# Moving transposes from TensorE to DMA and the norm to token rows, from batch 3 on, in a linear-attention plus feed-forward kernel

## Chip, cores, metric

One core of a Trainium2 chip. The metric is device time in microseconds of one execution; medians of several executions are quoted. Lower is better. An execution more than 1.5% above the fastest of the same kernel counts as slow and is left out.

## The reference

Eight batches of 8 heads, 576 tokens, 64 features per head. Attention has no softmax: per head `kv = k^T v`, `out = q kv`, then each token's 64 features are divided by their root mean square and multiplied by a gain. The 512 normed features of each of the 4608 tokens then pass a feed-forward layer of 2048 with a leaky activation.

```python
kv  = einsum('bhsd,bhse->bhde', k, v)
out = einsum('bhsd,bhde->bhse', q, kv)
out = out / sqrt(mean(out*out, -1) + 1e-6) * g_norm
h   = x @ w_in                      # x: 4608 x 512
y   = (max(h,0) + alpha*min(h,0)) @ w_out
```

## The kernel before

The feed-forward part runs in nine windows of 512 tokens. In window `w` the kernel interleaves 16 groups: four matmuls into `h_ps` (first layer), their eviction by ScalarE (`m_sb`) and VectorE (`gt`), and four matmuls into `y_ps` of the window before. After each group, at most a few attention "steps" of window `w + 1` are emitted; I call that place the group's **slot**. Every engine runs its instructions in the order in which they were emitted.

```python
def step_t(b, j):                     # q of a head pair, feature-major, by TensorE
    for t in range(NT):
        nc.tensor.matmul(out=qt_ps[:, t*P:(t+1)*P], lhsT=qs[:, t, 2*j:2*j+2, :],
                         rhs=ident16[:], is_transpose=True, ...)
    nc.vector.tensor_copy(out=qts[b, j][:], in_=qt_ps[:, 0:S])

def step_kv(b, j):                    # five matmuls, then VectorE masks into kvs[b, j]
    ...
def step_ot(w, j):                    # attention output, features on partitions
    nc.tensor.matmul(out=ot_ps[...], lhsT=kvs[b, j][:], rhs=qts[b, j][...], ...)
    nc.scalar.activation(out=sq[:], in_=ot_ps[:], func=AF.Square)

def step_ssq(w, j):                   # sums of squares by a matmul with a mask of ones
    nc.tensor.matmul(out=ssq_ps[:], lhsT=mask16[:], rhs=sq[:], ...)
    # ScalarE: Ln, Exp on 128x512;  VectorE: xts[w, j] = ot_ps * gain * rstd
# ... (cut)
for w in range(1, NW):
    steps = window_steps(w + 1)
    if 1 < w and w + 2 < B:
        load_batch(w + 2); regroup_batch(w + 2)      # GpSimd: loads, then copies
    for g in range(NF):                               # NF = 16
        m1_group(w, g)                                # 4 matmuls + eviction
        # ... y_mm x 4 of window w-1, y_out every fourth group
        want = n * (g - first_g + 1) // (NF - 2 - first_g)
        while steps and n - len(steps) < want:
            steps.pop(0)()                            # the slot
```

Of the kernel before, what the change touches and what calls it, by code (L numbers as in the profile page):

```python
# [9 lines left out]
FP32 = mybir.dt.float32  # L10
FP16 = mybir.dt.float16
AF = mybir.ActivationFunctionType
ALU = mybir.AluOpType
# [4 lines left out]
def kernel(  # L18
# [11 lines left out]
    nc = tc.nc  # L30

    B, H, S, D = q.shape
# [3 lines left out]
    P = 128  # L36
    NPAIR = H // 2
    W = 512
    NW = N_TOK // W
    TPW = W // P  # L40
    TPP = S // P
    MAIN = TPP * P
    REM = S - MAIN
    NT = TPP + 1
    NF = D_FF // P
    NC = D_MODEL // P
    assert NC == NPAIR and 0 < REM < P
    inv_d = 1.0 / D

    const_p = ctx.enter_context(tc.tile_pool(name="constp", bufs=1))  # L50
    w_p = ctx.enter_context(tc.tile_pool(name="weights", bufs=1))
    xt_p = ctx.enter_context(tc.tile_pool(name="xt", bufs=3))
    qkv_p = ctx.enter_context(tc.tile_pool(name="qkv", bufs=1))
    stage_p = ctx.enter_context(tc.tile_pool(name="stage", bufs=2))
    attn_p = ctx.enter_context(tc.tile_pool(name="attn", bufs=2))
# [2 lines left out]
    ps_h = ctx.enter_context(tc.tile_pool(name="psh", bufs=3, space=bass.MemoryType.PSUM))  # L58
    ps_y = ctx.enter_context(tc.tile_pool(name="psy", bufs=1, space=bass.MemoryType.PSUM))
    ps_s = ctx.enter_context(tc.tile_pool(name="pss", bufs=1, space=bass.MemoryType.PSUM))  # L60
    ps_o = ctx.enter_context(tc.tile_pool(name="pso", bufs=2, space=bass.MemoryType.PSUM))
    ps_q = ctx.enter_context(tc.tile_pool(name="psq", bufs=1, space=bass.MemoryType.PSUM))

    ctx.enter_context(
        tc.manual_schedule(engines={ENG.PE, ENG.Activation, ENG.DVE, ENG.Pool, ENG.SP})
# [7 lines left out]
            name=nc.get_next_instruction_name(),  # L73
# [14 lines left out]
    mask16 = const_p.tile([P, P], FP16, name="mask16")  # L88
# [3 lines left out]
    eps_t = const_p.tile([P, 1], FP32, name="eps_t")  # L92
# [3 lines left out]

    alpha_row = const_p.tile([NF, P], FP32, name="alpha_row")
    nc.sync.dma_start(out=alpha_row[:], in_=moe_alpha[:].rearrange("(g p) -> g p", p=P))
    g2col = const_p.tile([P, 1], FP32, name="g2col")
    nc.sync.dma_start(out=g2col[0:64, :], in_=g_norm[:].unsqueeze(1))  # L100
    nc.sync.dma_start(out=g2col[64:128, :], in_=g_norm[:].unsqueeze(1))
# [5 lines left out]
    NBUF = 3  # L107
    bufs = []
    for i in range(NBUF):
        t = {}  # L110
# [22 lines left out]
    def regroup(b, nm, h0, h1, eng=None):  # L133
        dst = bufs[b % NBUF][nm][:, 0:TPP, h0:h1, :].rearrange("p t h d -> p h t d")
        src = stages[b, nm][:, h0:h1, :, :]
        if eng is nc.scalar:
            nc.scalar.copy(out=dst, in_=src)
        else:
            (eng or nc.vector).tensor_copy(out=dst, in_=src)  # L139

    def load_batch(b, names=("k", "v", "q")):
        for nm in names:
            load_rem(b, nm)
            load_main(b, nm, 0, H)

    def regroup_batch(b):
        for nm in ("k", "v", "q"):
            regroup(b, nm, 0, H, nc.gpsimd)
# [24 lines left out]
    def w_in_blk(c, g):  # L173
        i, r = divmod(g, GW)
        return w_in_sb[i][:, c, r * P : (r + 1) * P]
# [22 lines left out]
    def keep_warm(n):  # L198
# [7 lines left out]
        out=alpha_ps[:], lhsT=alpha_row[:], rhs=ident[0:NF, 0:NF], is_transpose=True,  # L206
        start=True, stop=True,
# [4 lines left out]
        out=beta_sb[:], in0=alpha_ps[:], scalar1=-1.0, scalar2=1.0, op0=ALU.mult, op1=ALU.add,  # L212
# [3 lines left out]
    qts, kvs, xts = {}, {}, {}  # L216
# [16 lines left out]
    def step_kv(b, j, pool=(ps_s, "s")):  # L233
        ks, vs = bufs[b % NBUF]["k"], bufs[b % NBUF]["v"]
        kv_ps = pool[0].tile([P, P], FP32, name="kv_ps", tag=pool[1])
        for t in range(NT):
            nc.tensor.matmul(  # L237
                out=kv_ps[:],
                lhsT=ks[:, t, 2 * j : 2 * j + 2, :],
                rhs=vs[:, t, 2 * j : 2 * j + 2, :],  # L240
                start=(t == 0),
                stop=(t == NT - 1),
            )
        kvs[b, j] = attn_p.tile([P, P], FP16, name="kv_sb", tag=f"kv{j}")
        nc.vector.tensor_mul(out=kvs[b, j][:], in0=kv_ps[:], in1=mask32[:])  # L245


    ots = {}

    def step_ot(w, j):  # L250
        ot_ps = ps_o.tile([P, W], FP32, name="ot_ps", tag="o")
        n0 = w * W
        while n0 < (w + 1) * W:
            b = n0 // S
            n1 = min((b + 1) * S, (w + 1) * W)
            nc.tensor.matmul(  # L256
                out=ot_ps[:, n0 - w * W : n1 - w * W], lhsT=kvs[b, j][:],
                rhs=qts[b, j][:, n0 - b * S : n1 - b * S], start=True, stop=True,
            )
            n0 = n1  # L260
        sq = attn_p.tile([P, W], FP16, name="sq_sb")
        nc.scalar.activation(out=sq[:], in_=ot_ps[:], func=AF.Square)  # L262
        ots[w, j] = (ot_ps, sq)

    def step_ssq(w, j):
        ot_ps, sq = ots.pop((w, j))
        ssq_ps = ps_q.tile([P, W], FP32, name="ssq_ps", tag="q")
        nc.tensor.matmul(out=ssq_ps[:], lhsT=mask16[:], rhs=sq[:], start=True, stop=True)  # L268
        rstd = attn_p.tile([P, W], FP32, name="rstd")
        nc.scalar.activation(  # L270
            out=rstd[:], in_=ssq_ps[:], func=AF.Ln, bias=eps_t[:], scale=inv_d,
        )
        nc.scalar.activation(out=rstd[:], in_=rstd[:], func=AF.Exp, bias=0.0, scale=-0.5)  # L273
        xts[w, j] = xt_p.tile([P, W], FP16, name="xt", tag=f"xt{j}")
        nc.vector.scalar_tensor_tensor(  # L275
            out=xts[w, j][:], in0=ot_ps[:], scalar=g2col[:], in1=rstd[:],
            op0=ALU.mult, op1=ALU.mult,
        )

    def window_steps(w):  # L280
        f = []
        for j in range(NPAIR):
            f.append(("t", j))
            if j > 0:
                f.append(("ot", j - 1))
            f.append(("kv", j))
            if j > 0:
                f.append(("ssq", j - 1))
        f += [("ot", NPAIR - 1), ("ssq", NPAIR - 1)]
        if w >= B:  # L290
            f = [x for x in f if x[0] in ("ot", "ssq")]
        fn = {"t": step_t, "kv": step_kv, "ot": step_ot, "ssq": step_ssq}
        return [lambda n=n, j=j: fn[n](w, j) for n, j in f]
# [4 lines left out]
    def m1_mm(h_ps, w, g, cs):  # L298
        for c in cs:
            nc.tensor.matmul(  # L300
                out=h_ps[:], lhsT=w_in_blk(c, g), rhs=xts[w, c][:],
                start=(c == 0), stop=(c == NC - 1),
            )

# [10 lines left out]
    def m1_group(w, g):  # L315
        h_ps = ps_h.tile([P, W], FP32, name="h_ps", tag="h")
        m1_mm(h_ps, w, g, range(NC))
        m1_evac(h_ps, w, g)
# [8 lines left out]
    def y_out(y, w, a):  # L327
        y_sb = ysb_p.tile([P, D_MODEL], FP32, name="y_sb")
        nc.scalar.copy(out=y_sb[:], in_=y[:])  # L329
        i = 0  # L330
        while i < P:
            b, r = divmod(w * W + a * P + i, S)
            if r < MAIN:
                t, p = divmod(r, P)
                cnt = min(P - i, P - p)
                rows = out[b * S : b * S + MAIN, :].rearrange("(p t) m -> t p m", t=TPP)
                dst = rows[t, p : p + cnt, :]
            else:
                cnt = min(P - i, S - r)
                dst = out[b * S + r : b * S + r + cnt, :]  # L340
            nc.sync.dma_start(out=dst, in_=y_sb[i : i + cnt, :])
            i += cnt
# [19 lines left out]
    first = [ps_h.tile([P, W], FP32, name="h_ps", tag="h") for g in range(3)]  # L362
    for g in range(3):
        m1_mm(first[g], 0, g, (0, 1))
    step_ssq(0, 2)
    step_ssq(0, 3)
    for g in range(3):
        m1_mm(first[g], 0, g, (2,))
# [15 lines left out]
    steps = window_steps(1)  # L384
# [8 lines left out]
        f()  # L393

    for w in range(1, NW):
        steps = window_steps(w + 1) if w + 1 < NW else []
        n = len(steps)
        first_g = 4 if w == 1 else 0
        if 1 < w and w + 2 < B:
            load_batch(w + 2)  # L400
            regroup_batch(w + 2)
        y = None
        for g in range(NF):
            if w == 1 and g == first_g - 1:
                for nm in ("q", "k", "v"):
                    regroup(2, nm, 0, H)
                load_batch(3)
                regroup_batch(3)
            m1_group(w, g)
            if w > 1:  # L410
                a, part = divmod(g, TPW)
                if part == 0:
                    y = ps_y.tile([P, W], FP32, name="y_ps", tag="y")
                for gg in range(part * TPW, (part + 1) * TPW):
                    y_mm(y, w - 1, a, gg)
                if part == TPW - 1:
                    y_out(y, w - 1, a)

            want = n * (g - first_g + 1) // (NF - 2 - first_g)
            while steps and n - len(steps) < want:  # L420
                steps.pop(0)()
# [35 lines left out]
```

## Time and profile before

| what | before |
|---|---|
| median time | 329.7 us (329.2 to 330.5, 3 runs) |
| profiled span, clock | 328.0 us, 0.99 |
| TensorE, VectorE, ScalarE, GpSimd busy | 91, 49, 53, 23% |
| one window with a full set of steps | 32.44 us |

How to read it: the lines of the page, and what each of them says, are in the prediction below. A busy share is an average over the whole run; the figure that carries the argument is the issue spacing on TensorE inside one window, read from the timeline.

### The profile page before, as it was taken

What the parts mean: (1) busy time and instruction counts of PE and PEld (TensorE: products, weight loads), DVE (VectorE), ACT (ScalarE), POOL (GpSimd) and SP (SyncE); (2) the same over time, 40 slices, a digit from 0 to 9 for tenths busy, and PEclk for the clock granted to TensorE, in tenths of its full rate; (3) what the DMA queues carried; (4) which work ended last, traced back from release to release, by engine and by line L of the source; (5) the groups of instructions that cost most, each with busy time, mean ns of one, the idle gap of its engine ahead of it and who ended that gap; (6) DMA issues with size and microseconds to landing.
All of it is one profiled execution on the core that took longest, in us unless ns stands there. A gap on an engine that the chain in (4) does not pass through costs nothing.

```text
span 328.0 us, 4205 instructions
## 1 busy us (share of the span) xinstructions
PE 298.4 (91%) x1593; PEld 143.7 (44%) x1593; DVE 160.2 (49%) x271; ACT 173.4 (53%) x291; POOL 74.7 (23%) x80
## 2 busy tenths in 40 slices
PE   5657998768799999999999999999999999999994
PEld 1323354234355545544555455445544444444441
DVE  4247833285665545555455545554555455444300
ACT  2366605635846564657456745674557576544311
POOL 9723442765542055105500000000000000000000
PEclk9999999798999999999999999999999999999999
DMA  7999999996391199109901111101000211000132
GB/s 95 193 203 202 198 195 191 223 145 83 38 178 33 34 126 154 34 33 149 134 32 34 32 32 34 51 13 53 36 23 21 59 38 34 32 32 34 44 86 64
DMA packets 47621, 28.07 MB, mean 86 GB/s; under 512 B 14304, under 2 KB 42992, under 8 KB 47600
## 3 DMA queue, kind: packets, MB, share of 16 engines
q0 software_dynamic: 41904, 18.35, 44.5%
q1 hardware_dynamic: 5696, 9.45, 10.2%
q8 instruction: 12, 0.20, 0.3%
q14 instruction: 9, 0.07, 0.1%
HBM read 36.71 MB, written 9.44 MB: 141 GB/s over the span
## 4 chain that ended last, share of the span: by engine, by line
PE 83%; ACT 7%; DVE 4%; DMA 2%; issue 1%; POOL 1%; POOLq 0%; ACTq 0%
PE h_ps L300 36%; PE y_ps L322 34%; PE kv_ps L237 3%; PE ssq_ps L268 2%; PE qt_ps L222 2%; PE ot_ps L256 2%; ACT rstd L270 2%; DMA qsb<-in_q_dram 2%; ACT rstd L273 2%; DVE xt L275 1%; DVE gt L309 1%; ACT sq_sb L262 1%; ACT m_sb L307 1%; PE yd L322 1%; DVE qt_sb L231 1%
## 5 line engine op out<-in xcount | busy, mean ns | idle before, releaser
L300 PE MATMUL h_ps<-xt,w_in_sb 128*128 128x512 f16 x576 | 147.3, 384 | 4.1 <-ACT y_sb L329 1.5
L309 DVE SCALAR_TENSOR_TENSOR gt<-m_sb,beta_sb,h_ps 128x512 f16<-128x512 f32 x144 | 106.8, 745 | 88.4 <-ACT m_sb L307 86.9
L307 ACT ACTIVATE m_sb<-h_ps 128x512 f32<-128x512 f32 x144 | 85.1, 593 | 83.7 <-PE h_ps L300 83.6
L322 PE MATMUL y_ps<-w_out_sb,gt 128*128 128x512 f16 x512 | 128.8, 379 | 0.0
L322 PEld LDWEIGHTS <-gt 128*128 128x128 f16 x576 | 56.0, 98 | 67.5 <-issue 2.3
L300 PEld LDWEIGHTS <-w_in_sb 128*128 128x128 f16 x576 | 54.9, 99 | 67.2 <-issue 14.5
L275 DVE SCALAR_TENSOR_TENSOR xt<-ot_ps,g2col,rstd 128x512 f16<-128x512 f32 x36 | 27.0, 751 | 46.5 <-ACT rstd L273 46.5
L270 ACT ACTIVATE rstd<-ssq_ps,eps_t 128x512 f32<-128x512 f32 x36 | 24.7, 686 | 18.2 <-PE ssq_ps L268 18.2
L262 ACT ACTIVATE sq_sb<-ot_ps 128x512 f16<-128x512 f32 x36 | 21.3, 597 | 22.6 <-PE ot_ps L256 22.1
L329 ACT COPY y_sb<-y_ps 128x512 f32<-128x512 f32 x32 | 18.7, 585 | 18.4 <-PE y_ps L322 18.4
L273 ACT ACTIVATE rstd<-rstd 128x512 f32<-128x512 f32 x36 | 22.7, 629 | 1.1
L268 PE MATMUL ssq_ps<-sq_sb,mask 128*128 128x512 f16 x36 | 13.6, 378 | 7.0 <-ACT sq_sb L262 5.5
L222 PE MATMUL qt_ps<-ident,qsb 128*128 128x128 f16 x160 | 14.8, 227 | 5.7 <-DVE qsb L139 4.8
L237 PE MATMUL kv_ps<-vsb,ksb 128*128 128x128 f16 x160 | 14.5, 226 | 4.7 <-DVE qt_sb L231 4.7
L222 PEld LDWEIGHTS <-qsb 128*128 128x128 f16 x160 | 11.8, 101 | 13.5 <-DVE qsb L139 5.9
L231 DVE COPY qt_sb<-qt_ps 128x576 f16<-128x576 f16 x32 | 14.3, 451 | 6.4 <-PE qt_ps L222 6.3
L237 PEld LDWEIGHTS <-ksb 128*128 128x128 f16 x160 | 11.9, 101 | 12.1 <-issue 6.1
L256 PE MATMUL ot_ps<-qt_sb,kv_sb 128*128 128x512 f16 (+7 forms) x64 | 14.2, 296 | 0.3 <-DVE kv_sb L245 0.3
L128 POOL DMA_DIRECT2D ksb<-in_k_dram x8 | 5.6, 700 | 36.4 <-PE kv_ps L237 27.8
L139 POOL COPY ksb<-kst 128x2048 f16<-128x2048 f16 x5 | 9.5, 1893 | 18.7 <-DMA kst<-in_k_dram 18.7
L139 POOL COPY qsb<-qst 128x2048 f16<-128x2048 f16 x5 | 9.5, 1894 | 7.4 <-DMA qst<-in_q_dram 7.4
L139 POOL COPY vsb<-vst 128x2048 f16<-128x2048 f16 x5 | 9.5, 1894 | 6.8 <-DMA vst<-in_v_dram 6.8
(44 smaller groups left out, 111.6 us busy)
## 6 DMA issues: line engine op xcount, KB each, us to landing
out_dram<-y_sb SPq DMA_DIRECT2D x40, 128.0 KB, 2.3
out_dram<-y_sb SPq DMA_DIRECT2D x16, 256.0 KB, 2.3
kst<-in_k_dram POOLq DMA_DIRECT2D x7, 512.0 KB, 8.6
vst<-in_v_dram POOLq DMA_DIRECT2D x7, 512.0 KB, 10.1
qst<-in_q_dram POOLq DMA_DIRECT2D x7, 512.0 KB, 12.0
w_in_sb<-in_moe_w_in_dram POOLq DMA_DIRECT2D x4, 512.0 KB, 10.9
w_out_sb<-in_moe_w_out_dram POOLq DMA_DIRECT2D x4, 512.0 KB, 16.5
kst<-in_k_dram POOLq DMA_DIRECT2D x2, 256.0 KB, 5.5
```

The lines of the kernel that those rows point to most:

```text
L139: (eng or nc.vector).tensor_copy(out=dst, in_=src)
L222: nc.tensor.matmul(out=qt_ps[:, t * P : (t + 1) * P], lhsT=qs[:, t, 2 * j : 2 * j + 2, :], rhs=ident16[:], is_transpose=True, start=(t == ...
L237: nc.tensor.matmul(out=kv_ps[:], lhsT=ks[:, t, 2 * j : 2 * j + 2, :], rhs=vs[:, t, 2 * j : 2 * j + 2, :], start=(t == 0), stop=(t == NT - 1),)
L256: nc.tensor.matmul(out=ot_ps[:, n0 - w * W : n1 - w * W], lhsT=kvs[b, j][:], rhs=qts[b, j][:, n0 - b * S : n1 - b * S], start=True, stop=True,
L262: nc.scalar.activation(out=sq[:], in_=ot_ps[:], func=AF.Square)
L270: nc.scalar.activation(out=rstd[:], in_=ssq_ps[:], func=AF.Ln, bias=eps_t[:], scale=inv_d,)
L273: nc.scalar.activation(out=rstd[:], in_=rstd[:], func=AF.Exp, bias=0.0, scale=-0.5)
L275: nc.vector.scalar_tensor_tensor(out=xts[w, j][:], in0=ot_ps[:], scalar=g2col[:], in1=rstd[:], op0=ALU.mult, op1=ALU.mult,)
L300: nc.tensor.matmul(out=h_ps[:], lhsT=w_in_blk(c, g), rhs=xts[w, c][:], start=(c == 0), stop=(c == NC - 1),)
L307: nc.scalar.activation(out=m_sb[:], in_=h_ps[:], func=AF.Relu, scale=-1.0)
L309: nc.vector.scalar_tensor_tensor(out=gt[:], in0=m_sb[:], scalar=beta_sb[:, g : g + 1], in1=h_ps[:], op0=ALU.mult, op1=ALU.add,)
L322: nc.tensor.matmul(out=y[:], lhsT=gts[w, g][:, a * P : (a + 1) * P], rhs=w_out_blk(g), start=(g == 0), stop=(g == NF - 1),)
```

## The change

The intent is to free TensorE of work that is not the feed-forward. From batch 3 on, q is transposed by a DMA; the attention output is computed with tokens on partitions, so that a token's square sum is a row sum on VectorE; GpSimd builds `rstd * gain`; the normed rows go back to feature-major by DMA transposes into `xm`.

```diff
+    NB_PE = 3
-    ps_o = ...(name="pso", bufs=2)   # and ps_q, bufs=1
+    ps_o = ...(name="pso", bufs=1)   # tags o0, o1, o2
+    def transpose_q(b):
+        nc.sync.dma_start_transpose(out=qtms[b][:], in_=bufs[b % NBUF]["q"][:]...)
+    def tile_a(b, t):                 # one tile of 128 tokens, 8 heads
+        ot_ps = ps_o.tile([P, H, D], FP32, tag=f"o{n_tile[0] % 3}")
+        for j in range(NPAIR):
+            nc.tensor.matmul(out=ot_ps[:, 2*j:2*j+2, :], lhsT=qtms[b][:, t*NPAIR+j, :], rhs=kvs[b, j][:])
+        nc.scalar.activation(out=sq[0:n], in_=ot_ps[0:n], func=AF.Square)
+    def tile_b(b, t): ...             # VectorE tensor_reduce: ss
+    def tile_c(b, t): ...             # ScalarE Ln, Exp on 128x8; GpSimd rg = ss * g_all
+    def tile_d(b, t):
+        nc.vector.tensor_mul(out=x[0:n], in0=ot_ps[0:n], in1=rg[0:n])
+        nc.sync.dma_start_transpose(out=xm(w)[:, :, c:c+m], in_=x[i:i+m]...)
... (cut: the tail of batch 2, the list of tiles of a phase)
+            for k, fn in ((3, tile_d), (0, tile_a), (1, tile_b), (2, tile_c)):
+                if 0 <= i - k < len(seq): m.append(fn of seq[i - k])
+            if i < lead: m += first[:cut]           # kv steps, up to two in a slot
...
-        steps = window_steps(w + 1) if w + 1 < NW else []
+        steps = phase_steps(w + 1)
+            if g == NF - 3 and max(w + 2, NB_PE) < B and w + 2 >= NB_PE:
+                transpose_q(w + 2)
```

More of the change, by code (lines that the diff above doesn't have):

```diff
@@ L48 @@
     inv_d = 1.0 / D
+    NB_PE = 3
     const_p = ctx.enter_context(tc.tile_pool(name="constp", bufs=1))
     w_p = ctx.enter_context(tc.tile_pool(name="weights", bufs=1))
-    xt_p = ctx.enter_context(tc.tile_pool(name="xt", bufs=3))
+    xt_p = ctx.enter_context(tc.tile_pool(name="xt", bufs=2))
+    xm_p = ctx.enter_context(tc.tile_pool(name="xm", bufs=3))
     qkv_p = ctx.enter_context(tc.tile_pool(name="qkv", bufs=1))
@@ L60 @@
     ps_s = ctx.enter_context(tc.tile_pool(name="pss", bufs=1, space=bass.MemoryType.PSUM))
-    ps_o = ctx.enter_context(tc.tile_pool(name="pso", bufs=2, space=bass.MemoryType.PSUM))
-    ps_q = ctx.enter_context(tc.tile_pool(name="psq", bufs=1, space=bass.MemoryType.PSUM))
+    ps_o = ctx.enter_context(tc.tile_pool(name="pso", bufs=1, space=bass.MemoryType.PSUM))
     ctx.enter_context(
@@ L98 @@
     nc.sync.dma_start(out=alpha_row[:], in_=moe_alpha[:].rearrange("(g p) -> g p", p=P))
+    g_all = const_p.tile([P, D], FP32, name="g_all")
+    nc.sync.dma_start(out=g_all[:], in_=g_norm[:].partition_broadcast(P))
     g2col = const_p.tile([P, 1], FP32, name="g2col")
@@ L248, with xt_of @@
     ots = {}
+    xms = {}
+    def xt_of(w, c):
+        return xms[w][:, c, :] if w >= NB_PE else xts[w, c][:]
     def step_ot(w, j):
-        ot_ps = ps_o.tile([P, W], FP32, name="ot_ps", tag="o")
+        ot_ps = ps_o.tile([P, W], FP32, name="ot_ps", tag=f"o{j % 2}")
         n0 = w * W
@@ L266, in step_ssq @@
         ot_ps, sq = ots.pop((w, j))
-        ssq_ps = ps_q.tile([P, W], FP32, name="ssq_ps", tag="q")
+        ssq_ps = ps_o.tile([P, W], FP32, name="ssq_ps", tag="o2")
         nc.tensor.matmul(out=ssq_ps[:], lhsT=mask16[:], rhs=sq[:], start=True, stop=True)
@@ L278, in step_ssq, with step_tail_ot @@
         )
+    TAIL = NB_PE * (S - W)
+    JT = min(NPAIR, W // TAIL)
+    def step_tail_ot(i):
+        ot_ps = ps_o.tile([P, JT, TAIL], FP32, name="ot_ps", tag=f"o{i % 2}")
+        for u in range(JT):
+            j = i * JT + u
+            nc.tensor.matmul(
+                out=ot_ps[:, u, :], lhsT=kvs[NB_PE - 1, j][:],
+                rhs=qts[NB_PE - 1, j][:, S - TAIL : S], start=True, stop=True,
+            )
+        sq = attn_p.tile([P, JT, TAIL], FP16, name="sq_sb")
+        nc.scalar.activation(out=sq[:], in_=ot_ps[:], func=AF.Square)
+        ots["tail", i] = (ot_ps, sq)
@@ new lines, in step_tail_ssq @@
+    def step_tail_ssq(i):
+        ot_ps, sq = ots.pop(("tail", i))
+        ssq_ps = ps_o.tile([P, JT, TAIL], FP32, name="ssq_ps", tag="o2")
+        nc.tensor.matmul(out=ssq_ps[:], lhsT=mask16[:], rhs=sq[:], start=True, stop=True)
+        rstd = attn_p.tile([P, JT, TAIL], FP32, name="rstd")
+        nc.scalar.activation(
+            out=rstd[:], in_=ssq_ps[:], func=AF.Ln, bias=eps_t[:], scale=inv_d,
+        )
+        nc.scalar.activation(out=rstd[:], in_=rstd[:], func=AF.Exp, bias=0.0, scale=-0.5)
+        nc.vector.scalar_tensor_tensor(
+            out=xm(NB_PE)[:, i * JT : (i + 1) * JT, 0:TAIL], in0=ot_ps[:], scalar=g2col[:],
+            in1=rstd[:], op0=ALU.mult, op1=ALU.mult,
+        )
@@ new lines, with xm @@
+    qtms, tiles = {}, {}
+    def xm(w):
+        if w not in xms:
+            xms[w] = xm_p.tile([P, NPAIR, W], FP16, name="xm")
+        return xms[w]
+    def transpose_q(b):
+        qtms[b] = attn_p.tile([P, NT * NPAIR, P], FP16, name="qtm")
+        nc.sync.dma_start_transpose(
+            out=qtms[b][:], in_=bufs[b % NBUF]["q"][:].rearrange("p t h d -> p (t h d)"),
+        )
+    n_tile = [0]
+    def tile_a(b, t):
+        ot_ps = ps_o.tile([P, H, D], FP32, name="otm_ps", tag=f"o{n_tile[0] % 3}")
+        n_tile[0] += 1
+        for j in range(NPAIR):
+            nc.tensor.matmul(
+                out=ot_ps[:, 2 * j : 2 * j + 2, :], lhsT=qtms[b][:, t * NPAIR + j, :],
+                rhs=kvs[b, j][:], start=True, stop=True,
+            )
+        n = P if t < TPP else REM
+        sq = attn_p.tile([P, H, D], FP32, name="sqm_sb", tag="rstd")
+        nc.scalar.activation(out=sq[0:n], in_=ot_ps[0:n], func=AF.Square)
+        tiles[b, t] = [n, ot_ps, sq]
@@ new lines, in tile_b, with tile_c @@
+    def tile_b(b, t):
+        n, _, sq = tiles[b, t]
+        ss = attn_p.tile([P, H], FP32, name="ss", bufs=3)
+        nc.vector.tensor_reduce(
+            out=ss[0:n], in_=sq[0:n], op=ALU.add, axis=mybir.AxisListType.X,
+        )
+        tiles[b, t][2] = ss
+    def tile_c(b, t):
+        n, _, ss = tiles[b, t]
+        nc.scalar.activation(
+            out=ss[0:n], in_=ss[0:n], func=AF.Ln, bias=eps_t[0:n], scale=inv_d,
+        )
+        nc.scalar.activation(out=ss[0:n], in_=ss[0:n], func=AF.Exp, bias=0.0, scale=-0.5)
+        rg = attn_p.tile([P, H, D], FP32, name="rg")
+        nc.gpsimd.tensor_tensor(
+            out=rg[0:n], in0=ss[0:n].unsqueeze(2).to_broadcast([n, H, D]),
+            in1=g_all[0:n].unsqueeze(1).to_broadcast([n, H, D]), op=ALU.mult,
+        )
+        tiles[b, t][2] = rg
@@ new lines, in tile_d, with phase_steps @@
+    def tile_d(b, t):
+        n, ot_ps, rg = tiles.pop((b, t))
+        x = attn_p.tile([P, H, D], FP16, name="xrow", bufs=3)
+        nc.vector.tensor_mul(out=x[0:n], in0=ot_ps[0:n], in1=rg[0:n])
+        i = 0
+        while i < n:
+            w, c = divmod(b * S + t * P + i, W)
+            m = min(n - i, W - c)
+            nc.sync.dma_start_transpose(
+                out=xm(w)[:, :, c : c + m], in_=x[i : i + m].rearrange("p h d -> p (h d)"),
+            )
+            i += m
+    def phase_steps(w):
+        if w < NB_PE:
+            return window_steps(w)
+        if w >= NW:
+            return []
+        todo = [(b, t) for b in range(NB_PE, min(B, w + 1)) for t in range(NT)
+                if (b, t) not in done and b * S + t * P < (w + 1) * W]
+        done.update(todo)
+        old = [x for x in todo if x[0] < w]
+        new = [x for x in todo if x[0] == w]
+        pre = []
+        if w == NB_PE:
+            n = NPAIR // JT
+            pre = [lambda i=i: step_tail_ot(i) for i in range(n)] + [
+                lambda i=i: step_tail_ssq(i) for i in range(n)]
+        kv = [lambda j=j: step_kv(w, j) for j in range(NPAIR)] if w < B else []
+        first = []
+        for i in range(max(len(pre), len(kv))):
+            first += kv[i : i + 1] + pre[i : i + 1]
+        seq = old + new
+        lead = len(old)
+        steps = []
+        if lead == 0:
+            steps += [[f] for f in first]
+            first = []
+        for i in range(len(seq) + 3):
+            m = []
+            for k, fn in ((3, tile_d), (0, tile_a), (1, tile_b), (2, tile_c)):
+                if 0 <= i - k < len(seq):
+                    m.append(lambda fn=fn, x=seq[i - k]: fn(*x))
+            if i < lead:
+                cut = -(-len(first) // (lead - i))
+                m += first[:cut]
+                first = first[cut:]
+            steps.append(m)
+        return [lambda m=m: [f() for f in m] for m in steps]
@@ L280, in window_steps @@
+    done = set()
     def window_steps(w):
@@ L300, in m1_mm @@
             nc.tensor.matmul(
-                out=h_ps[:], lhsT=w_in_blk(c, g), rhs=xts[w, c][:],
+                out=h_ps[:], lhsT=w_in_blk(c, g), rhs=xt_of(w, c),
                 start=(c == 0), stop=(c == NC - 1),
```

## The prediction

> **What bounds the kernel now.** I read the page first (busy shares and slices), then the groups, then the waits, then a timeline of one group slot.
>
> ```profile
> PE 298.4 (91%) x1593; PEld 143.7 (44%) x1593; DVE 160.2 (49%) x271; ACT 173.4 (53%) x291; POOL 74.7 (23%) x80
> PE   5657998768799999999999999999999999999994
> POOL 9723442765542055105500000000000000000000
> DMA  7999999996391199109901111101000211000132
> ```
>
> TensorE is at 9 tenths from 90 us to the end, with every other engine near half. The DMA engines are nearly idle in the second half, which is the room that the change wants to use.
>
> ```profile
> L300 PE MATMUL h_ps<-xt,w_in_sb 128*128 128x512 f16 x576 | 147.3, 384 | 4.1 <-ACT y_sb L329 1.5
> L322 PE MATMUL y_ps<-w_out_sb,gt 128*128 128x512 f16 x512 | 128.8, 379 | 0.0
> L275 DVE SCALAR_TENSOR_TENSOR xt<-ot_ps,g2col,rstd 128x512 f16<-128x512 f32 x36 | 27.0, 751 | 46.5 <-ACT rstd L273 46.5
> L268 PE MATMUL ssq_ps<-sq_sb,mask 128*128 128x512 f16 x36 | 13.6, 378 | 7.0 <-ACT sq_sb L262 5.5
> L222 PE MATMUL qt_ps<-ident,qsb 128*128 128x128 f16 x160 | 14.8, 227 | 5.7 <-DVE qsb L139 4.8
> ```
>
> The two big matmul groups wait only 4.1 us in all. Their "mean ns" must not be added up, since neighbours overlap in the pipeline; the timeline gives the issue spacing:
>
> ```profile
> 189.10 0.44 PE L222 MATMUL qt_ps<-ident,qsb 128*128 128x128 f16 x5
> 189.38 1.03 PE L300 MATMUL h_ps<-xt,w_in_sb 128*128 128x512 f16 x4
> 190.24 1.03 PE L322 MATMUL y_ps<-w_out_sb,gt 128*128 128x512 f16 x4
> 190.44 0.60 ACT L307 ACTIVATE m_sb<-h_ps 128x512 f32<-128x512 f32 x1 [1.41 <-PE h_ps L300]
> 191.07 0.75 DVE L309 SCALAR_TENSOR_TENSOR gt<-m_sb,beta_sb,h_ps 128x512 f16<-128x512 f32 x1 [0.89 <-ACT m_sb L307]
> 191.11 0.44 PE L237 MATMUL kv_ps<-vsb,ksb 128*128 128x128 f16 x5
> ```
>
> Four 512-column matmuls take 0.864 us (189.38 to 190.24), so 0.216 each; five of 128 columns take 0.28, so 0.055 each. TensorE runs its instructions in program order, so an attention step sits in the "slot" after the y matmuls (here 191.11). The eviction of the same group ends on VectorE at 191.82, **0.71 us after that slot opens**. That number matters below.
>
> ```profile
> PE ssq_ps L268 <- ACT sq_sb L262: 5.5, 7, 1.2
> SPq L341 <- ACT y_sb L329: 243.8, 30, 59.5
> ```
>
> The square-sum matmul after the last ot step in windows 1 to 6 already stalls TensorE (0.69 us of recorded idle, 0.85 between issues). The output queue is nearly all waiting, so it has room.
>
> By the timeline, windows 2 to 6 last 32.44 us each (window 3 from 122.5 to 154.95) and window 7, without transposes and kv, 29.35. My sum for one: 128 big matmuls x 0.216 = 27.65, q transposes 20 x 0.055 = 1.08, kv 1.08, ot about 0.87, ssq 4 x 0.216 = 0.86, stall 0.85 to 0.9: 32.4. It closes, so TensorE's instruction stream is the time, and any idle put into it is lost one for one.
>
> **What the skill says.** "VectorE: DVE Perf Modes", The three transpose paths: a 128x128 16-bit transpose is 390 ns on TensorE and 1309 ns through the DMA crossbar. The trace agrees that TensorE is cheap: 0.055 us each in a stream. No DMA transpose is in this trace. "DMA: Bandwidth & Descriptors", Latency and other measured facts: 261 GB/s effective for a DMA transpose; its Anatomy of one DMA: about 2.0 us fixed. The fixed part agrees: the y stores take 2.3 us from issue to landing. "GPSIMD Engine Reference", 3.1: a two-input tensor_tensor of 2048 fp32 is 4497 ns; no such operation is in the trace, but a one-input copy of 2048 is 1.89 us here. "Perfetto Trace Analysis", Identifying Performance Opportunities: repeating bubbles on the saturated engine can mean too few PSUM buffers; that is what I expect the change to create.
>
> **Part by part.**
>
> *TensorE work removed.* Window 2 prepares batch 3 and window 3, and so on; windows 2 to 7 change. Windows 3 and 5 have 4 token tiles of 4 x 128 columns: 27.65 + 1.08 + 4 x 0.216 = 29.6, gain 2.85 each. Windows 4 and 6 have 5 tiles: 29.8, gain 2.65 each. Window 2 has 3 tiles and the tail of batch 2 (4 x 192 and 2 x 384 columns, 0.65): 30.0, gain 2.4. Window 7: 28.5, gain 0.85. Sum **14.2 us**, of which the vanished ssq stalls are over 4. Without new waits the result would be 329.7 - 14.2 = 315.5.
>
> *Evictions.* ScalarE loses most of 24 x (0.69 + 0.63) us of Ln and Exp on 512 columns; VectorE swaps 20 copies of 0.45 and 22 products of 0.75 for 25 row sums and 25 products, estimated 0.65 to 0.7 each (its 128-column product is 0.285). Both stay near half busy. Worth nothing by itself.
>
> *GpSimd.* 25 products of 512 elements: a quarter of the skill's figure is 1.1 us, estimate 1.3. They stand in queue behind load and regroup, which took 15 to 18 us in the trace (114.5 to 132.7). The loads can start when the previous phase's last product is done, some 7 to 8 us before the window ends, so the queue is free 8 to 11 us into the window; the first product is wanted at group 5, about 11 us in. Just in time, so I charge nothing, with a risk of a few us.
>
> *New wait 1: PSUM for the token tiles.* There are three ot buffers. From the fourth tile of a phase, tile i needs the buffer that the product of tile i-3 frees, and that product is emitted **in the same slot**. VectorE reaches it 0.71 us after the slot opens, takes 0.69, so TensorE waits about 1.42 us. Tiles beyond the third: 1, 2, 1, 2, 1 in windows 3 to 7, so 7 x 1.42 = **9.9 us**.
>
> *New wait 2: two kv steps in one slot* with one buffer. The second waits for the masked product of the first, which is behind the eviction (0.71) and perhaps a row sum (0.65). TensorE gets there 0.49 us into the slot and is released at 1.06 or 1.68. Window 3 has it twice (0.57 and 1.2), windows 4 and 5 once (0.57): about **2.9 with window 6 rounded in** at 0.5.
>
> *New wait 3: the start of each window.* The last tile of a phase is multiplied in the slot of group 13 and is ready 1.40 us into it. The next window's first matmul comes after two more groups, 4 x 0.864 = 3.46 us in. So the transpose has 2.06 us to land. Estimated at 131 KB / 261 GB/s + 2.0 = 2.5 us, it is late by 0.45 us even on an empty queue (windows 6 and 7). In windows 2 to 5 the q transpose of a later batch, 655 KB or 2.5 us by the same rate, is issued just ahead of it on the same queue; and the POOL loads start at the same time (through window 4), so the rate may halve. With 7 steps spread over the groups (windows 3, 5) q goes out two groups earlier, with 8 or 14 (windows 4, 2) only one. Estimates: window 2 4.5, window 3 3, window 4 4.5, window 5 0.7, windows 6 and 7 0.5 each: **13.7 us**, the softest number here.
>
> Sum: 315.5 + 9.9 + 2.9 + 13.7 = **342.0 us**.
>
> **Rivals.**
> *Clean gain.* Transposes land in time and the PSUM wait is shorter than I read it: 315 to 323 us. For it: the DMA slices are at 0 to 2 tenths late in the run, and the y store's landing of 2.3 us nearly fits. Against: wait 1 follows from program order alone, and needs no DMA figure.
> *Same.* Waits 1 and 2 as worked out, but the DMA side costs under 1 us a window: 329 to 333. For it: the q transpose might be fully drained before the last tile is ready.
> *DMA transposes are slow.* If a transpose goes block by block near the skill's 1.3 us, then 20 blocks of q are 26 us and four of a tile over 5; each window start then waits 5 us or more, and the last tiles queue behind q: 355 to 380. For it: the rate is measured on another kernel.
> *GpSimd late.* If the product of the first tile is behind the regroup, VectorE stalls at its product, the h buffers fill, and three windows lose 2 to 4 us: 350.
>
> **Range and chances.** The centre is 342. Waits 1 and 2 are within some 4 us; wait 3 could be 4 or 30. Low end 326 (a third of wait 3, part of wait 1 hidden), high end 360 (transposes twice as slow). Faster than 323 needs two of my steps to fail: 0.08. Within 2% (323.1 to 336.3): 0.27. Slower: 0.65.
>
> **What would show it.** Right: about 100 fewer transposes at L222 and some 22 fewer ssq matmuls; in the waits, TensorE's token-tile matmuls released by VectorE's x product, 7 times at about 1.4 us; kv matmuls released by the kv_sb product some 4 times; h_ps matmuls released by a DMA onto xm once a window, longest in windows 2 to 4. Granted clock still 0.99 to 1. Wrong: no DMA wait ahead of h_ps (the transposes are fast, then near 329 or less), no wait of the tiles on VectorE (then 10 us less), or h_ps waits on VectorE behind GpSimd (then rival four).

## The result

The changed kernel takes **369.7 us** (368.5 to 371.1, 4 runs) against 329.5 us of the kernel before in the same rounds: ratio 1.122, 95% interval 1.116 to 1.128. A ratio here is the mean time of one kernel's fast runs over that of the other's of the same rounds, so it is not quite the ratio of the quoted medians. The direction was predicted; the time lies above the stated range of 326 to 360.

The page of the changed kernel, its busy shares, and the slices of TensorE, its clock, GpSimd and DMA:

```profile
PE 298.0 (81%) x1531; PEld 139.0 (38%) x1531; DVE 167.4 (45%) x279; ACT 156.7 (42%) x300; POOL 100.7 (27%) x105
PE   5668997777999328895697905989988998999994
POOL 8633344623003432134412534021012103100000
PEclk9696999989999859999699965999999999999999
DMA  6999999694022990129902499124111311310033
```

Where the kernel before had an unbroken row of nines, TensorE now has three holes (slices with 3 and 2, with 5 and 6, with 0 and 5). In each hole DMA is at 9 tenths, and in each the granted clock falls. Past the third hole the run is again at 8 or 9 until its last slice.

The groups and the waits, then the landing times of the two kinds of transposes. In a wait line the figures are microseconds in total, times, and the longest; in an issue line the last figure is the median time to landing:

```profile
L225 PE MATMUL qt_ps<-ident,qsb 128*128 128x128 f16 x60 | 6.0, 241 | 7.1 <-DVE qsb L142 6.1
L338 PE MATMUL otm_ps<-kv_sb,qtm 128*128 128x128 f16 x100 | 9.7, 219 | 8.7 <-DVE xrow L371 8.7
...
PE h_ps L441 <- issue: 25.2, 2, 13.1
PE otm_ps L338 <- DVE xrow L371: 8.7, 7, 1.3
PE h_ps L441 <- DMA xm<-xrow: 8.4, 2, 7.5
PE kv_ps L240 <- DVE kv_sb L248: 2.0, 4, 0.9
...
xm<-xrow SPq DMA_TRANSPOSE x28, 2.4
qtm<-qsb SPq DMA_TRANSPOSE x5, 13.8
```

The work that should go has gone: 60 transposes on TensorE in place of 160. The token tiles wait for the row product 7 times, as worked out, and kv on kv 4 times. The large item is `h_ps`: 33.6 us in four waits. Two of them are booked as "issue", because the profile found no event for them; the next view shows that the first of them ends with a landing of `xm`. A q transpose takes 13.8 us to land in the median, where I had estimated about 4.5.

The timeline of the changed kernel around the start of window 3, first the output queue (SPq), the start of the loads (POOL) and then TensorE at the starts of windows 3 to 6:

```profile
117.73 2.55 SPq L376 DMA_TRANSPOSE xm<-xrow  x2
119.34 0.74 POOL L131 DMA_DIRECT2D ksb<-in_k_dram  x1
120.38 7.15 SPq L328 DMA_TRANSPOSE qtm<-qsb  x1
127.62 2.50 SPq L376 DMA_TRANSPOSE xm<-xrow  x2
...
135.83 1.86 PE L441 MATMUL h_ps<-xm,w_in_sb 128*128 128x512 f16 x4 [13.06 <-issue]
178.22 1.86 PE L441 MATMUL h_ps<-xm,w_in_sb 128*128 128x512 f16 x4 [7.49 <-DMA xm<-xrow]
225.21 1.87 PE L441 MATMUL h_ps<-xm,w_in_sb 128*128 128x512 f16 x4 [12.17 <-issue]
259.73 1.02 PE L441 MATMUL h_ps<-xm,w_in_sb 128*128 128x512 f16 x4 [0.91 <-DMA xm<-xrow]
```

The q transpose occupies the queue for 7.15 us, so the last token tile is issued at 127.6 and not at about 121. It is split in two at the border of the windows; the piece that window 3 reads takes 8.1 us to land (the view of DMA issues for 127.5 to 128.5 alone), which is 135.7, and window 3 begins at 135.83. The fourth start, 259.73, is the one whose q transpose had no load beside it: 4.1 us to landing for q, 2.4 for the token tile, and a stall of 0.91.

The first four matmuls after the three long stalls take 1.86 us in place of 1.02: half clock. The Trainium skill says this in "TensorE: Matmul & The Clock Gate", Part 1: after an idle stretch of about 3.4 us the clock gate passes half the pulses until TensorE has been busy for about as long. The traces agree roughly: 1.86 after every stall of 5 us or more, 1.02 after 0.91. The granted clock was 0.50 for another 4.3, 2.9 and 3.7 us after the three long stalls had ended. From the start of a window to its first token tile the timeline has 5.57, 4.87 and 5.26 us after the long stalls and 3.45 after the short one, so the slow stretches cost 2.1 + 1.4 + 1.8 = 5.3 us; half of the time at half clock would be nearly the same, 5.5.

### The profile page after: what moved, and what is told of

Read it like the earlier page. It is cut to its first block, busy times and chain, and to the rows that moved or that the text cites. A ratio compares the mean times of both kernels' runs of the same rounds, so it can differ in the third digit from the quotient of the medians.

```text
span 369.1 us, 4224 instructions
## 1 busy us (share of the span) xinstructions
PE 298.0 (81%) x1531; PEld 139.0 (38%) x1531; DVE 167.4 (45%) x279; ACT 156.7 (42%) x300; POOL 100.7 (27%) x105
## 3 DMA queue, kind: packets, MB, share of 16 engines
q1 hardware_dynamic: 31216, 15.71, 19.9%
## 4 chain that ended last, share of the span: by engine, by line
PE 68%; DMA 9%; ACT 7%; issue 7%; DVE 7%; POOL 1%; SPq 0%; POOLq 0%; ACTq 0%
PE h_ps L441 33%; PE y_ps L463 26%; DMA qtm<-qsb 4%; ACT m_sb L448 3%; DMA xm<-xrow 3%; PE kv_ps L240 2%; DVE gt L450 2%; ACT rstd L277 2%; DMA qsb<-in_q_dram 2%; PE otm_ps L338 2%; ACT rstd L280 1%; DVE xrow L371 1%; DVE xt L282 1%; DVE qt_sb L234 1%; PE yd L463 1%
## 5 line engine op out<-in xcount | busy, mean ns | idle before, releaser
L441 PE MATMUL h_ps<-xm,w_in_sb 128*128 128x512 f16 x384 | 101.7, 388 | 33.8 <-issue 25.2
L362 POOL TENSOR_TENSOR rg<-ss,g_all 128x512 f32<-128x512 f32 (+1 forms) x25 | 26.0, 1041 | 140.6 <-ACT ss L360 100.7
L441 PE MATMUL h_ps<-xt,w_in_sb 128*128 128x512 f16 x192 | 50.3, 403 | 3.5 <-ACT y_sb L470 1.5
L344 ACT ACTIVATE sqm_sb<-otm_ps 128x512 f32<-128x512 f32 (+1 forms) x25 | 14.9, 597 | 16.7 <-PE otm_ps L338 16.7
L282 DVE SCALAR_TENSOR_TENSOR xt<-ot_ps,g2col,rstd 128x512 f16<-128x512 f32 x12 | 9.0, 751 | 18.1 <-ACT rstd L280 18.1
L371 DVE TENSOR_TENSOR xrow<-otm_ps,rg 128x512 f16<-128x512 f32 (+1 forms) x25 | 17.0, 682 | 0.0
L350 DVE TENSOR_REDUCE ss<-sqm_sb 128x8 f32<-128x512 f32 (+1 forms) x25 | 16.9, 675 | 0.0
L338 PE MATMUL otm_ps<-kv_sb,qtm 128*128 128x128 f16 x100 | 9.7, 219 | 8.7 <-DVE xrow L371 8.7
L269 ACT ACTIVATE sq_sb<-ot_ps 128x512 f16<-128x512 f32 x12 | 7.0, 593 | 15.5 <-PE ot_ps L263 15.5
L225 PE MATMUL qt_ps<-ident,qsb 128*128 128x128 f16 x60 | 6.0, 241 | 7.1 <-DVE qsb L142 6.1
## 6 DMA issues: line engine op xcount, KB each, us to landing
qst<-in_q_dram POOLq DMA_DIRECT2D x7, 512.0 KB, 14.2
```

What stands on the lines that cost most here:

```text
L338: nc.tensor.matmul(out=ot_ps[:, 2 * j : 2 * j + 2, :], lhsT=qtms[b][:, t * NPAIR + j, :], rhs=kvs[b, j][:], start=True, stop=True,)
L344: nc.scalar.activation(out=sq[0:n], in_=ot_ps[0:n], func=AF.Square)
L350: nc.vector.tensor_reduce(out=ss[0:n], in_=sq[0:n], op=ALU.add, axis=mybir.AxisListType.X,)
L362: nc.gpsimd.tensor_tensor(out=rg[0:n], in0=ss[0:n].unsqueeze(2).to_broadcast([n, H, D]), in1=g_all[0:n].unsqueeze(1).to_broadcast([n, H, D ...
L371: nc.vector.tensor_mul(out=x[0:n], in0=ot_ps[0:n], in1=rg[0:n])
L441: nc.tensor.matmul(out=h_ps[:], lhsT=w_in_blk(c, g), rhs=xt_of(w, c), start=(c == 0), stop=(c == NC - 1),)
```

## The experiments

Theory A: the last token tile of a window lands late because the q transpose of a later batch is ahead of it in the same queue, and the loads that GpSimd starts at the same time stretch that q transpose. Rivals: the loads alone do it (B), the q transpose alone does it (C), or the waits inside the windows matter more than the window starts. In the edits below, lines are joined and shortened. e1, e5, e6 and the changed kernel form a square: load beside the last token tile or not, q ahead of it or not.

| run | median us (range) | ratio to before, 95% | stalls at the starts of windows 3, 4, 5, 6 |
|---|---|---|---|
| changed kernel (load and q) | 369.7 (368.5 to 371.1) | 1.122 (1.116 to 1.128) | 13.06, 7.49, 12.17, 0.91 |
| e1 q early (load only) | 353.5 (353.4 to 354.4) | 1.074 (1.069 to 1.079) | 5.64, 5.12, 5.13, 0.27 |
| e5 load late (q only) | 346.9 (346.2 to 347.9) | 1.054 (1.048 to 1.059) | 5.92, 2.01, 3.19, 1.37 |
| e6 both (neither) | 336.7 (334.3 to 338.5) | 1.020 (1.012 to 1.029) | 2.71, 0.27, 0.72, 0.28 |
| e4 bank wait away | 353.7 (351.1 and 356.4, fast runs alone) | 1.074 (1.062 to 1.086) | 9.15, 5.50, 6.53, 0.98 |
| e3 q by DMA only | 333.6 (331.1 to 334.9) | 1.011 (1.005 to 1.017) | none |
| e10 the same, q at group 8 | 326.3 (326.1 to 327.5) | 0.990 (0.987 to 0.994) | none |
| e9 before, steps spread | 323.9 (323.4 to 326.6) | 0.984 (0.979 to 0.990) | none |
| e8 grid | **317.2 (316.8 to 317.9)** | **0.962 (0.957 to 0.967)** | none |
| e12 grid, loads early | 329.3 (327.8 to 330.9) | 1.000 (0.995 to 1.006) | 3.27, 0.74, 3.39, none |

The nine experiments are recorded as giving correct outputs. The stalls are the recorded idle of TensorE in the profiled run.

### e1: the q transpose moved away

```diff
-            if g == NF - 3 and max(w + 2, NB_PE) < B and w + 2 >= NB_PE:
+            if g == 8 and max(w + 2, NB_PE) < B and w + 2 >= NB_PE:
```

> The q transpose is issued at group 8 instead of group 13, so the last token tile of a window no longer has it ahead in the queue; the loads still start near the window's end. Theory A (the last token tile lands late because the q transpose, stretched by the loads running beside it, is ahead of it in the same queue): the three long window-start stalls of 13.1, 7.5 and 12.2 us fall to 2 us or less each, the half-clock stretches after them go, 334 to 340 us. Rival B (the loads alone make the token transpose slow, the order in the queue does not matter): stalls of 6 us or more stay, 352 us or more.

It took 353.5 us. The window starts of e1:

```profile
125.93 1.86 PE L441 MATMUL h_ps<-xm,w_in_sb 128*128 128x512 f16 x4 [5.64 <-DMA xm<-xrow]
166.37 1.86 PE L441 MATMUL h_ps<-xm,w_in_sb 128*128 128x512 f16 x4 [5.12 <-DMA xm<-xrow]
```

A stall of 5 us stays with no q ahead at all. The last token tiles still took 7.3 to 7.8 us to land. So theory A as I had put it missed: the loads alone stretch even the small token transposes, and the time is the one expected of rival B (whose stalls of 6 us or more were not quite reached). But the q transpose ahead was worth 16 us too, so B alone does not describe it either. Clear of the loads, the four q transposes of windows 2 to 5 held the queue for 2.4 to 3.6 us.

### e5: the loads held back

A one-column copy on GpSimd that reads the window's first activation goes ahead of the loads, and the regroup copies move into the window. Holding the issue of the loads by real data keeps the program free of races.

```diff
-        if 1 < w and w + 2 < B: load_batch(w + 2); regroup_batch(w + 2)   # at the window's head
+            if late and g == 1:
+                nc.gpsimd.tensor_copy(out=gate[:], in_=gts[w, 0][:, 0:1])
+                load_batch(w + 2)
+            if late and g in RG:      # {8: k, 10: v and q}
+                for nm in RG[g]: regroup(w + 2, nm, 0, H, nc.gpsimd)
```

> The q transpose stays at group 13, but the loads of the batch after next are held until the second group of a window (a one-column copy of that window's first activation goes ahead of them on GpSimd), so no load runs beside the transposes. Theory A: a q transpose lands in about 4 us as the one without a load beside it did (4.1), window starts stall 0.5 to 3 us each, 338 to 346 us. Rival C (the q transpose is slow by itself and merely being ahead is enough): stalls of 7 us or more stay, 358 us or more.

It took 346.9 us, 0.9 above the expected span. The q transposes landed in 4.9 to 5.8 us and held the queue for 3.0 to 4.0 us; the token tiles behind them landed in 2.3 to 3.1 us. Two of the window starts:

```profile
162.97 1.14 PE L441 MATMUL h_ps<-xm,w_in_sb 128*128 128x512 f16 x4 [2.01 <-DMA xm<-xrow]
201.25 1.86 PE L441 MATMUL h_ps<-xm,w_in_sb 128*128 128x512 f16 x4 [3.19 <-DMA qtm<-qsb]
```

Stalls of 2.01, 3.19 and 1.37 us are those of q alone. The 5.92 at window 3 has a second cause, which e6 shows alone.

### e6: neither

```diff
-            if g == NF - 3 ...: transpose_q(w + 2)          # before the slot
+            if g == NF - 1 ...: transpose_q(w + 2)          # after the slot of the last group
```

> Loads held as in e5, and the q transpose issued after the last group, so the last token transpose meets neither. Theory A: the token transpose lands in 2.3 to 2.4 us, window starts stall 0.5 us or less, clock 0.98 or more, 328 to 335 us; what is left against the zero-wait estimate are the PSUM and kv waits of 11 to 12 us. Rival B or C: if either load or q alone were enough, e1 and e5 would differ by more than 15 us, and this run equals the better of them.

It took 336.7 us, 1.7 above the expected span. Three of the four starts are clean (0.27, 0.72, 0.28). The first, 2.71, is of my own making. VectorE in window 2 of e6, and the stretch of e6 from 127.1 to 130.5 us (the 0.50 in it is the granted clock):

```profile
121.67 0.69 DVE L371 TENSOR_TENSOR xrow<-otm_ps,rg 128x512 f16<-128x512 f32 x1 [2.73 <-POOL rg L362]
...
127.10:130.50 3.40, 3.40 (x9) 1.21 (x8) 0.75 (x1) 0.71 (x2) 1.62 (x3) 0.50 0.87 179
```

The row product waited 2.73 us for GpSimd, where I had put the regroup copies among the products of the shortest phase. That is the "GpSimd late" rival of the prediction; it did not occur in the changed kernel, where the wait before that product is 0.0, but it does as soon as the copies are moved carelessly. e5 has the same 2.73 us. The second line shows that this stall too is followed by half clock, although its first four matmuls, begun at 126.06, still ran in 1.02 us: another 1.7 us by estimate.

The square now reads: 16 us go with q alone, 23 with the load alone, 33 with both. Neither is enough, and they overlap in part. The 23 and the 33 are somewhat too small, since e5 and e6 carry the self-made stall, some 4 us with its half clock by estimate, and the other two do not.

### e4: the PSUM wait alone

```diff
-            for k, fn in ((3, tile_d), (0, tile_a), (1, tile_b), (2, tile_c)):
+            for k, fn in ((2, tile_d), (0, tile_a), (1, tile_b), (1, tile_c)):
-        for i in range(len(seq) + 3):
+        for i in range(len(seq) + 2):
```

> Only the PSUM wait is taken away: the product of a tile is emitted two steps after the tile instead of three (row sums and rsqrt share a step), so a bank is free one step before it is wanted. Theory A: the 7 waits of token-tile matmuls on the row product, 8.7 us recorded and about 1.4 us each in issue time, go; the window-start stalls stay; 358 to 362 us. Rival (the waits are hidden, because the window then just waits longer for its transpose): 367 us or more.

The two fast executions took 351.1 and 356.4 us, below the expected span (with the two slow ones, 360.1 and 360.5, the median would be 358.2, inside it). The wait is gone from the group:

```profile
L338 PE MATMUL otm_ps<-kv_sb,qtm 128*128 128x128 f16 x100 | 9.7, 219 | 0.0
```

What this saves cannot be read from the time alone: the profiled execution is the fastest, with window starts 11 us better in sum than in the changed kernel. The step list is one shorter, so the q transpose and the loads meet at a slightly different moment: here the q transposes were through the queue in 2.5 to 3.1 us. Window 6, which has a long start stall in neither kernel, gives it directly: 30.46 us in e4 against 32.95, 2.5 us for two waits. In window 7 only 0.1 us is left of a wait of 1.2, because e4 has new stalls of up to 0.6 us there. So the waits are not hidden in window 6; for the others it is not shown.

Why the starts differ: all traces of this case fit one order. A q transpose issued before the first 512 KB load that runs beside it held the queue for 2.5 to 4.4 us, one issued after it, while loads were running, for 6.7 to 9.3 us (once, in e12, for 4.5). In the changed kernel q came 0.3 us before that load in window 3 (held 2.75 us, the smallest of the three long stalls) and 0.3 and 0.6 us after it in windows 2 and 4. No run moves the order alone, so this is seen and not tested.

### e3 and e10: only q by DMA

The other half of the change, on the kernel before: batches 3 to 7 take q from the DMA transpose; ot, square sum and norm stay as they were.

```diff
+        if NB_PE <= w < B: f = [x for x in f if x[0] != "t"]
+                rhs = qtms[b][:, t:t + k, j, :]      # in step_ot, in place of qts[b, j]
+            if g == NF - 3 ...: transpose_q(w + 2)   # e10: g == 8
```

> Half of the change alone: q of batches 3 to 7 is transposed by DMA at group 13 and read by the old feature-major steps; the norm stays as it was, with the ones-mask matmul, so no window waits for a token transpose. Theory A: the 100 TensorE transposes (5.4 us) and, because 12 steps spread over 14 groups no longer share the last slot, five of the 0.85 us stalls of the square-sum matmul go; the q transpose has a whole window to land and costs nothing; 319 to 323 us. Rival (a q transpose costs TensorE or the loads something wherever it stands): 327 us or more.

It took 333.6 us: a miss. The two culprits:

```profile
131.92 0.37 PE L265 MATMUL ot_ps<-qtm,kv_sb 128*128 128x256 f16 x1 [4.92 <-DMA qtm<-qsb]
169.13 0.32 PE L265 MATMUL ot_ps<-qtm,kv_sb 128*128 128x128 f16 x2 [5.20 <-DMA qtm<-qsb]
```

I had given q "a whole window to land". It had not: the first ot step of the next window came up at 127.0, 11 us after the issue at 115.8, and the median of the five q transposes, three of them beside a load, was 16.0 us.

> The run with the q transposes alone missed (333.6 instead of 319 to 323): two ot matmuls waited 4.9 and 5.2 us for a q transpose that had taken 15 us or more beside a load. Here only its place moves, from group 13 to group 8, clear of the loads. Theory A as mended (a transpose beside a load lands several times later; without one it costs TensorE nothing): the waits go, the q transpose lands in 4 to 6 us, 319 to 323 us. Rival (the strided reads of q by the ot matmuls or the transposes as such cost 10 us): 329 us or more.

It took 326.3 us, still above the expected span. One wait of 4.21 us is left, in window 4, and the q transpose of window 3 was not where the edit had put it:

```profile
161.71 0.32 PE L265 MATMUL ot_ps<-qtm,kv_sb 128*128 128x128 f16 x2 [4.21 <-DMA qtm<-qsb]
...
SPq L254 <- PE ot_ps L265: 24.4, 3, 8.6
...
146.47 7.91 SPq L254 DMA_TRANSPOSE qtm<-qsb  x1
```

Group 8 of window 3 begins at 136.55, but SyncE issued q at 146.47: it waited 8.6 us for the last ot matmul that still read the buffer to be overwritten (`qtm` has two). By then a batch's load had started at 142.9, and the transpose held the queue for 7.91 us. The issue is 9.9 us after the start of group 8, as it is in e3, whose edit says group 13. The same wait stands in windows 4 and 5. So of these windows e10 moves q in time in window 2 alone, where the wait of e3 has gone, and it tests its two theories only there.

### e9: what has nothing to do with transposes

```diff
             want = n * (g - first_g + 1) // (NF - 2 - first_g)
+            if w > 1 and n == 16 and 7 <= g < 13:
+                want += 1
```

> The kernel before with nothing of the change, only the order in time of its attention steps moved so that the last ot and the last square sum of windows 2 to 6 do not share a slot. It says how much of the gain of e3 or e8 has nothing to do with transposes. Five stalls of 0.85 us go: 324 to 326 us; if the stall were hidden elsewhere, 329.

It took 323.9 us. The five stalls of the square-sum matmul in windows 2 to 6 are gone from the trace. So 1.6% was to be had in the kernel before by an edit of two lines, and counts as part of what the change removes: of the 13.2 us by which e8 beats the kernel before in the same rounds, 6.4 are reached by e9 too.

### e8 and e12: the change without its waits

e8 keeps every part of the change and places it otherwise: tile `i` at group `g0 + 2i`, its row sum one group later, its `rstd` two, its product four; one kv step in a slot; loads held to group 1, regroup copies at 7, 9 and 11; q after the last group.

```diff
+        for i, x in enumerate(todo):
+            put(g0 + 2 * i + 4, tile_d, *x)
+        for i, x in enumerate(todo):
+            put(g0 + 2 * i, tile_a, *x)
+            put(g0 + 2 * i + 1, tile_b, *x)
+            put(g0 + 2 * i + 2, tile_c, *x)
+        for j in range(NPAIR): put(j, step_kv, w, j)
+    RG = {7: ("k",), 9: ("v",), 11: ("q",)}
```

> The whole change with every wait that theory A names taken away: loads held to the second group and q last as in e6, the tiles on a fixed grid of groups so that a bank is free a group before it is wanted, one kv step a slot, the last product at group 10 to 12 instead of 13. Theory A: no wait of the tiles on the product, no wait of kv on kv, window starts at 0.3 us or less; the zero-wait sum of the prediction, 315.5, plus up to 3 us: 315 to 319 us. Rival (something that neither theory names, a slower clock or GpSimd, eats the gain): 323 us or more.

It took **317.2 us**, 3.8% faster than the kernel before, and is the fastest kernel here. The groups of its page, and the start of window 3:

```profile
L456 PE MATMUL y_ps<-w_out_sb,gt 128*128 128x512 f16 x512 | 128.9, 379 | 0.0
L434 PE MATMUL h_ps<-xm,w_in_sb 128*128 128x512 f16 x384 | 98.6, 379 | 0.0
...
120.86 1.03 PE L456 MATMUL y_ps<-w_out_sb,gt 128*128 128x512 f16 x4
121.72 1.03 PE L434 MATMUL h_ps<-xm,w_in_sb 128*128 128x512 f16 x4
```

The `h_ps` matmuls that read transposed rows wait 0.0 us in all, where the changed kernel had 33.8 on that line. Window 4 begins at 151.38, so window 3 lasts 29.66 us, against 29.6 worked out for it without waits and 32.45 before. Transposes are not always fast in e8: beside its held loads, token tiles land in up to 9.2 us. They do so in the middle of a window, more than 6 us before the next window reads them, and cost nothing.

e12 puts one thing back into e8: the loads start as early as in the changed kernel, with their regroup copies right behind them.

> The fastest version so far with one thing put back: the loads are not held, so GpSimd starts them at the end of the window before, when the last tokens are transposed. The q transpose stays behind them. Theory A as mended: the last token tiles land in 7 to 8 us instead of 2.4, the 3.8 us that the grid leaves do not cover it, three windows start 3 to 4 us late and run at half clock for a moment: 327 to 334 us. Rival (with the grid and q last, the loads no longer matter): 320 us or less.

```profile
124.52 1.42 PE L434 MATMUL h_ps<-xm,w_in_sb 128*128 128x512 f16 x4 [3.27 <-DMA xm<-xrow]
156.74 1.02 PE L434 MATMUL h_ps<-xm,w_in_sb 128*128 128x512 f16 x4 [0.74 <-DMA xm<-xrow]
190.15 1.89 PE L434 MATMUL h_ps<-xm,w_in_sb 128*128 128x512 f16 x4 [3.39 <-DMA xm<-xrow]
```

It took 329.3 us, in the expected span: 12 us are lost to the place of the loads and their copies alone, although the grid gives the last tile 1.7 us more to land. The three recorded stalls make 7.4 us of it; the granted clock is at half for 3.4 us after the first and 3.1 us after the third, some 3.3 us more by estimate. I have not split the remaining 1 us.

## Why the prediction was wrong, point by point

The sum had four terms. Against the trace of the changed kernel:

| term of the prediction | predicted us | shown us | from |
|---|---|---|---|
| time with no new wait | 315.5 | 317.2 | e8 |
| wait 1, PSUM bank | 9.9 | 8.7 | 7 waits of 1.2 to 1.3 |
| wait 2, kv on kv | 2.9 | 2.0 | 4 waits of 0.38 to 0.90 |
| wait 3, window starts | 13.7 | 33.6 | 13.06 + 7.49 + 12.17 + 0.91 |
| half clock after stalls | 0 | 5.3 | three stretches, above |

- **Right: what bounds the kernel, and what the change takes off it.** The working from issue spacings gave 14.2 us. e8 has no wait left that the theory names, and comes within 1.7 us of the number.
- **Right: waits 1 and 2**, in count and nearly in size. (The terms of wait 2 for windows 3 to 5 add to 2.9 by themselves; with the 0.5 for window 6 the sum would be 3.4. The four waits fell in windows 3, 3, 4 and 5.) The recorded idle is some 0.2 us shorter than the wait between issues on which the prediction was worked out.
- **Right: GpSimd is in time in the changed kernel.** Its product takes 1.04 us (estimate 1.3), and no row product waited for it.
- **The failed step is wait 3 in windows 2, 3 and 4**, put as 4.5 + 3 + 4.5 = 12 us with the words "the rate may halve". The mechanism was the one named: the last token transpose misses a deadline of about 2 us, with q ahead of it and the loads beside it. The size was off, 32.7 us for these three. Two things stand in its place. First, beside a load a transpose takes some two and a half to four times as long: 7.3 to 8.9 us against 2.4 for a token tile (e1 and the changed kernel), 9.8 to 14.6 against 4.1 for q. I had halved only the rate of the bytes. Second, the q transposes of windows 2, 3 and 4 kept the issuing queue for 7.2, 2.8 and 6.7 us, and until then the next transpose is not even issued; I had counted q only as bytes ahead in the same queue.
- **Missing: the half clock.** The prediction treats a wait as lost one for one, and named a granted clock of 0.99 to 1 as a sign of being right; it was 0.93. After each of the three long waits it costs some 1.4 to 2.1 us on top. The page of the skill that says so was at hand and was not used.
- **The other windows were right**: 0.91 against 0.7 for the one with q but no load, and no recorded stall against 0.5 for the two with neither.
- **The rival "DMA transposes are slow" had the number (355 to 380) but not the cause**, so that its range holds the result is luck. A transpose by itself is as fast as estimated: 4.1 us against 4.5 for q, 2.4 against 2.5 for a token tile.

The shown terms add to 317.2 + 8.7 + 2.0 + 33.6 + 5.3 = 366.8 against 369.7. The last 2.9 us are not shown. Most of them may be the difference between recorded idle and issue time: 15 waits at the 0.16 us of the kernel before (0.69 recorded, 0.85 between issues) would be 2.4.

What also stays open is why a load stretches a transpose so much. The runs show that it does, and that a transpose away from the load is fast again (token tiles in e5, 2.3 to 3.1 us; the q transposes of windows 2 to 5 in e1, 4.2 to 5.2); whether it is the share of the 16 engines, the number of small packets, or the taking of turns between queues was not separated. The changed kernel moves 31,216 packets on the hardware queue in place of 5,696, for 6.26 MB more; in the trace 24,448 of the added packets have 256 bytes, the rest 4.

## What to carry to other kernels

Taking work off the bounding engine is worth its issue time only if the new path meets every deadline: write down for each new transfer when it is issued, what is ahead of it in its queue, what else runs on the DMA engines then, and when its reader comes. The same parts cost 12% in one placement and gave 4% in another. Before that, look for stalls already in the loop; here a reordering by two lines gave 1.6% by itself, about half of what the best version of the change gives. And check in the trace that an experiment happened when its edit says it should: in e10 it did not.

## What the Trainium skill lacked or had wrong

- "DMA: Bandwidth & Descriptors", Latency and other measured facts and Anatomy of one DMA: from 261 GB/s and 2.0 us fixed I had estimated 4.5 us for 655 KB and 2.5 us for 131 KB. Alone the runs show 4.1 and 2.4, so the sum holds within a tenth, although the 2.0 us stand there for DMAs issued from GpSimd and these are issued from SyncE. What it has no figure for is the case beside a load issued from GpSimd: up to 16.7 us for q (e3) and 9.2 for a token tile (e8). Its Rules for kernel authors say that "A transpose next to ordinary DMAs needs nothing", which is meant of the results, and holds for them here (eight runs with DMA transposes are correct), but not of the time.
- The same page has no figure for how long a transpose keeps the issuing queue beside a load. Here a token tile holds it for 1.2 us in the median, q for 2.4 to 4.0 us clear of a load and for up to 9.3 us beside one.
- "VectorE: DVE Perf Modes", The three transpose paths: 1309 ns for one 128x128 block by DMA. Four such blocks landed in 2.4 us and twenty in 4.1 us, so it must not be multiplied by the number of blocks; the page does not say so.
- "TensorE: Matmul & The Clock Gate", Part 1: about 3.4 us of idle brings the half clock. Here less was enough: after recorded stalls of 2.01 and 3.19 us (e5), 2.71 (e6) and 3.27 (e12) the granted clock was 0.50 for 3.4 us, and at the window starts with 1.37 us or less (e5 and others) it was not. It can set in about 1 us after the stall has ended, so the first four matmuls (1.14 and 1.02 us after 2.01 and 2.71) do not show it; ask for the granted clock of a stretch.
- "GPSIMD Engine Reference", 3.1: a quarter of its 4497 ns, my estimate for 512 elements, is 1.12 us; the product with two broadcast inputs took 1.04 us. Nothing is wrong here.
